# A seven-product form of the second matrix product in every second block, with one of its sums formed in place by transfers

## The chip, the cores and the metric

The kernel runs on one core of a Trainium2 chip. The metric is device time in microseconds (us) of one execution. Lower is better.

## The reference

`x` has 8 sequences of 4096 tokens with 192 features. A causal convolution of seven taps over the tokens, with softmax weights for each of 8 heads (24 features each), is followed by a two-layer network with an exact GELU and no bias:

```python
w = softmax(weight, axis=-1)                       # 8 x 7
x_unf = x_pad[:, arange(S)[:, None] + arange(7)]   # six zeros ahead of each sequence
h = einsum('hk,bskhg->bshg', w, x_unf)             # 32768 x 192
out = gelu(h @ w_in) @ w_out                       # 192 -> 2048 -> 192
```

Inputs and output are float32; the matrix products run in bfloat16.

## The kernel before

The 32768 tokens are two halves of 16384, and the kernel walks both at the same time: partitions 0 to 63 hold a third of the 192 features for the one half, partitions 64 to 127 for the other. A block `n` is 512 tokens of each half (256 in the first six), so there are 35 blocks. Every matmul from block 7 on works on 64x64 tiles, four of which run side by side on the 128x128 array. One call on each of the four tiles with 512 columns is called a *round* here.

The order on each engine is written by hand, and semaphores tie the engines together:

- **SyncE (SP)** loads `x` into three buffers `xin` and stores `osb`, in one list: load of a block ahead, store of the block before.
- **VectorE (DVE)** transposes the input (`trans`, L735), makes the taps of the convolution (`conv`, L756 and L763: `acc = xT * w + acc`, the last one into `xc` in bfloat16), and brings results out of PSUM by transposing them into `osb` (`evac_t`, L371). A tap is two calls, over 1024 and over 512 elements. The list `plan` has these steps of a block, and `side` sets other work between them: a step with the key (b, o, r) comes ahead of step o of block b.
- **ScalarE (ACT)** makes GELU, 16 calls of 1024 elements a block (slots, L910), each from one of two PSUM buffers `hp` into `gT`. For some blocks (`K0`) it also makes the first tap, in three calls (`first_tap`, L878) two blocks ahead, at the slots in `TAPS`.
- **TensorE (PE)** alternates in each slot of block `n` three rounds of the first product (`mm1`, L1005) and about three of the second product of block `n - 1` (L1085), so that a block has 48 + 48 rounds. `mm1` of a slot waits until the GELU of two slots before is done with its buffer.
- **GpSimd (POOL)** copies the halo of six tokens and issues the transfers of the sums.

In the blocks in `ST` (9, 12, ... 33) the second product has another form. Two token groups, pairs of chunks and two of the three output thirds make a 2x2x2 product, formed with seven products (P1 to P7) instead of eight; the last third (units D and E) is formed as before. So it takes 44 rounds (`A(h, par)` is the GELU output of token group h, for the chunks of parity par). It is in `mm2_s` (L1147), which follows the list `EVENTS`, made from `TILES`: a string for each of the four tiles, in which each unit (P1 to P7, D, E) is eight calls. `ROUNDS` says how many rounds stand in each slot. The form needs four sums of GELU outputs in bfloat16: S1, Dn, S4 and a quarter of S3 by DVE (`st_add`, L479 to L487), and three quarters of S3 by transfers (`st_dma`, L461 and L464: a copy into `sst`, then a second transfer that adds to it). The four PSUM banks in `ob` are called X, D, Y and V there. When products are done, ACT copies parts of X to SBUF (`st_copy`, L507, at `AT_COPY`), DVE makes corrections (`st_post`, L516 to L531) and transposes the results (`st_evac`, L543). In the block after a rewritten one, when TensorE makes these products, ACT makes copies and no first taps; DVE then makes the first tap of the block after next itself.

Of the kernel before, what the change touches and what calls it, by code (L numbers as in the profile page):

```python
# [11 lines left out]
def bass_lightweight_conv__then__act_gelu_exact_kernel(  # L12
# [80 lines left out]
    for m in range(M0, M1):  # L93
        if m in ST:
            BK[m] = dict(zip(("X", "D", "Y", "V"), FREE))
            FREE = [BK[m][k] for k in ("X", "V", "D", "Y")]
        else:
            BK[m] = FREE[:3]
            FREE = [FREE[3], *FREE[:3]]
# [22 lines left out]
    with es:  # L122
# [20 lines left out]
        wst = sbt("wst", [128, 4 * NF // 2 * 64], BF16)  # L143
        wot = sbt("wot", [128, NF * C], BF16)
        wtf = sbt("wtf", [128, NF // 2 * 64], F32)
        sst = [sbt("sst%d" % i, [128, NF // 2 * TB], BF16) for i in range(4)]
# [40 lines left out]
        S_SA = [sem("S_SA%d" % i) for i in range(4)]  # L187
        S_AC = sem("S_AC")
        S_DP = sem("S_DP")
        S_CP = [sem("S_CP%d" % q) for q in range(3)]  # L190
        S_AD = [sem("S_AD%d" % q) for q in range(3)]
# [61 lines left out]
        NCV = 2 * KS  # L253
# [29 lines left out]
        def cvd(n):  # L283

            return sum(NCV - 2 * (m in K0) for m in range(n + 1) if m not in PC)
# [15 lines left out]
        def wait_ev(e, m, g):  # L301

            if m < NA:
                e.wait_ge(S_EVA, G0[m] + g + 1)
            else:
                e.wait_ge(S_EV, EVC[m] + g + 1)

        def wait_banks(t, m, g):

            k = G0[m] + g  # L310
            if m < M0:
                if k >= 2:
                    t.wait_ge(S_EVA, k - 1)
            elif g % 2:
                t.wait_ge(S_GELU, SL0[NB] - 1 + g // 2)
            elif M1 - 1 in ST:
                i = ST.index(M1 - 1)
                t.wait_ge(*((S_AC, 6 * i + 4) if g == 0 else (S_EV, EVC[M1] - 2)))
                t.wait_ge(S_DP, 5 * i + 3 + g)
            else:  # L320
                t.wait_ge(S_EV, EVC[M1] - 2 + g)
# [42 lines left out]
        def evac_t(v, m, j):  # L364
# [8 lines left out]
        LO, UP = slice(0, 64), slice(64, 128)  # L373
        UNIT = {
# [3 lines left out]
        }  # L378
# [4 lines left out]
        NS, NE = ("S1", "S3", "Dn", "S4"), ("P1", "P5", "P7", "P3L", "P3U", "P6", "DE")  # L383

        EVENTS = []
        for (hf, cg), names in TILES.items():
            at = 0.0
            for u in names.split():
                d = 0.5 if u == "P3" else 1.0
                EVENTS += [(at + d * k / 8, hf, cg, u, k) for k in range(8)]  # L390
                at += d
        EVENTS.sort()
        GROUP = {}
        for e, (at, hf, cg, u, k) in enumerate(EVENTS):
            name = "DE" if u[0] in "DE" else u if u != "P3" else u + "LU"[cg]
# [3 lines left out]
        for e, (at, hf, cg, u, k) in enumerate(EVENTS):  # L399
# [4 lines left out]
            last[UNIT[u][0], cg] = e  # L404
        DONE = sorted(DONE)
        assert DONE[-1] < len(EVENTS) - 1
# [3 lines left out]
        def st_done(e, m, name):  # L410
            e.wait_ge(S_ST, len(DONE) * ST.index(m) + DONE.index(GROUP[name]) + 1)
# [4 lines left out]
        def weights(v, k):  # L416
# [6 lines left out]
            def w(i):  # L423
                return ap(wst, i * (NF // 2) * 64, [[4 * NF // 2 * 64, 128], [64, NF // 2], [1, 64]])
# [20 lines left out]
            elif k == 7:  # L445
                ins = v.tensor_tensor(w(3), b(1, 0), f, ALU.subtract)
            else:
                ins = v.tensor_tensor(w(2), b(0, 1), b(1, 1), ALU.subtract)
            ins.then_inc(S_WT)

        PART = {"S1": 4, "S3": 4, "Dn": 2, "S4": 2}
        ND = 3

        def st_dma(e, m, q, h):

            i, n = ST.index(m), NF // 2 // PART["S3"]
            dst = ap(sst[1], q * n * TB, [[NF // 2 * TB, 128], [TB, n], [1, TB]])
            src = ap(gT[m % 2], (4 * q * n + h) * TB, [[NF * 2 * TB, 128], [4 * TB, n], [1, TB]])
            if h == 0:
                e.wait_ge(S_GELU, SL0[m] + 2 * (q + 1) * n - 1)  # L460
                e.dma_start(dst, src).then_inc(S_CP[q], 16)  # L461
            else:
                e.wait_ge(S_CP[q], 16 * (i + 1))
                e.dma_start(dst, src, accum_op=ALU.add).then_inc(S_AD[q], 16)  # L464

        def st_add(v, m, name, q):

            g, n = gT[m % 2], NF // 2 // PART[name]

            def a(h, par):  # L470
                return ap(g, (2 * q * n + par) * 2 * TB + h * TB, [[NF * 2 * TB, 128], [4 * TB, n], [1, TB]])

            def t(k):
                return ap(sst[k], q * n * TB, [[NF // 2 * TB, 128], [TB, n], [1, TB]])

            i = ST.index(m)
            v.wait_ge(S_GELU, SL0[m] + 2 * (q + 1) * n)
            if name == "S1":
                ins = v.tensor_tensor(t(0), a(1, 0), a(1, 1), ALU.add)  # L479
            elif name == "S3":  # L480
                ins = v.tensor_tensor(t(1), a(0, 0), a(1, 0), ALU.add)
            elif name == "Dn":
                v.wait_ge(S_SA[0], PART["S1"] * i + (q + 1) * n * PART["S1"] // (NF // 2))
                ins = v.tensor_tensor(t(2), a(0, 0), t(0), ALU.add)
            else:
                v.wait_ge(S_SA[2], PART["Dn"] * i + q + 1)
                ins = v.tensor_tensor(t(3), a(0, 1), t(2), ALU.add)  # L487
            ins.then_inc(S_SA[NS.index(name)])

        def st_copy(a, m, k):  # L490

            def xb(r, w=TB):
                return bank(BK[m]["X"], r, w)

            if k > 3:
                a.wait_ge(S_AC, 6 * ST.index(m) + 4)
            if k in (0, 1, 3):
                st_done(a, m, ("P1", "P5", "", "P6")[k])
            dst, src = (
                (gsm[LO, :], xb(LO)),  # L500
                (p5s[UP, :], xb(UP)),
                (p5s[LO, 0 : TB // 2], xb(UP, TB // 2)),
                (uu[LO, :], xb(LO)),
                (uu[UP, :], uu[LO, :]),
                (gsm[UP, :], uu[LO, :]),
            )[k]
            a.activation(out=dst, in_=src, func=AF.Copy, scale=-1.0 if k > 3 else 1.0).then_inc(S_AC)  # L507

        def st_post(v, m, k):
            i = ST.index(m)  # L510
            hw = TB // 2
            vb = [bank(BK[m]["V"], r, hw) for r in (LO, UP)]
            if k == 0:
                st_done(v, m, "P7")
                v.wait_ge(S_AC, 6 * i + 2)
                ins = v.tensor_tensor(tq[UP, :], bank(BK[m]["Y"], UP), p5s[UP, :], ALU.subtract)  # L516
            elif k == 1:
                st_done(v, m, "P3L")
                v.wait_ge(S_AC, 6 * i + 3)
                ins = v.tensor_tensor(tq[LO, 0:hw], vb[0], p5s[LO, 0:hw], ALU.add)  # L520
            elif k == 2:
                st_done(v, m, "P3U")
                ins = v.tensor_tensor(tq[LO, hw:TB], vb[1], p5s[UP, hw:TB], ALU.add)
            elif k == 3:
                v.wait_ge(S_AC, 6 * i + 5)
                v.wait_ge(S_DP, 5 * i + 3)
                ins = v.tensor_tensor(tq[:, :], tq[:, :], uu[:, :], ALU.add)
            else:
                v.wait_ge(S_MM2, MMC[m + 1])
                v.wait_ge(S_AC, 6 * i + 6)  # L530
# [3 lines left out]
        def st_evac(v, m, j):  # L534
            i = ST.index(m)
            if j == 2:
                st_done(v, m, "DE")
                v.wait_ge(S_OUT[m % 2], OUTS[m - 2])
                src = bank(BK[m]["D"])
            else:  # L540
                v.wait_ge(S_DP, 5 * i + 5 - j)
# [15 lines left out]
        def store(e, m):  # L557
# [28 lines left out]
        TAPS = (7, 10, 12)  # L586
        AT_ST = {
            "S1": [(1, 9, 0), (2, 0, 0), (2, 1, 0), (2, 5, -1)],
            "S3": [(2, 5, 1)],
            "Dn": [(2, 0, 2), (2, 5, 2)],  # L590
            "S4": [(2, 0, 4), (2, 6, 0)],
            "post": [(2, 11, 0), (3, 0, 0), (3, 2, 0), (3, 6, 0), (3, 9, 0)],
            "ev": [(3, 10, 0), (3, 7, 0), (3, 4, 0)],
        }

        def at_ev(n):

            if n - 1 in ST:
                return [(2, 15, 0), (3, 4, 0), (3, 4, 0)]
            return [(2, 13, 0) if n == M0 else (3, 0, 3), (3, 5, 0), (3, 5, 0)]  # L600

        AT_COPY = {0: (1, 6), 1: (1, 8), 2: (1, 10), 3: (1, 13), 4: (2, 1), 5: (2, 4)}

        @block.gpsimd
        def _(g):
# [72 lines left out]
            for n in range(3, M1 + 2):  # L678
                if n < NB:
                    halo(n)  # L680
                if n - 2 in ST:
                    for q, h in ((0, 0), (1, 0), (0, 1), (2, 0), (1, 1), (2, 1)):
                        st_dma(g, n - 2, q, h)

        @block.vector
        def _(v):
# [50 lines left out]
            def conv(n, k, s):  # L737

                w = WS[n]
                h = int(n in K0)  # L740
                p0, pn = (0, 2) if s == 0 else (2, 1)
                if k == h and s == 0:
# [514 lines left out]
```

## Time and profile before

| | us |
|---|---|
| median of 3 runs | 671.52 |
| lowest and highest | 671.3, 672.17 |
| the profiled execution | 671.6 |
| its span in the profile | 669.9 |
| PE busy in the span | 666.3 |
| DVE busy | 596.7 |
| ACT busy | 587.4 |
| POOL busy | 90.4 |

The span runs from the first to the last instruction that the profile shows; the time also holds what lies around it. PE is TensorE's matmuls, PEld its weight loads, which overlap with them. A row of a view names the line in the kernel, the engine, the operation, the tiles as out<-in, and the shape.

### The profile page before, as it was taken

The numbers are of one execution on the slowest core, as the hardware profiler recorded it, in microseconds if no ns is written. First come the engines' busy times: TensorE is split into PE (matmuls) and PEld (weight loads), VectorE is DVE, ScalarE is ACT, GpSimd is POOL, SyncE is SP. The second block draws the span as 40 slices with busy tenths as digits, with TensorE's granted clock in tenths as the row PEclk, the third lists the DMA queues.
The fourth block names the chain that finished last, engine by engine and source line by source line (L and its number), as shares of the span: only waits on it lengthen the run. The fifth ranks groups of instructions, "written<-read, shape, count | busy, mean of one in ns | idle before, by whom it ended". The sixth has DMA issues, their size and how long they took to land.

```text
span 669.9 us, 27227 instructions
## 1 busy us (share of the span) xinstructions
PE 666.3 (99%) x12504; PEld 407.7 (61%) x12504; DVE 596.7 (89%) x706; ACT 587.4 (88%) x659; POOL 90.4 (13%) x115
## 2 busy tenths in 40 slices
PE   9999999999999999999999999999999999999998
PEld 8999655556555555655565555556555655555567
DVE  5989999899999989998999999999999999998633
ACT  8988988889988998998899889888989998898783
POOL 7020000030012003001300120030013001200300
PEclk9999999999999999999999999999999999999999
DMA  9535234263466048515634660475156346602423
GB/s 150 125 88 130 61 72 96 69 134 88 96 138 143 10 96 175 112 38 129 135 84 97 141 141 7 96 175 112 42 134 131 80 97 141 144 4 64 115 63 96
DMA packets 142786, 67.82 MB, mean 101 GB/s; under 512 B 127248, under 2 KB 140880, under 8 KB 142672
## 3 DMA queue, kind: packets, MB, share of 16 engines
q1 hardware_dynamic: 129136, 49.37, 32.6%
q0 software_dynamic: 12416, 16.13, 12.0%
q8 instruction: 98, 1.61, 1.0%
q10 hardware_dynamic: 1120, 0.59, 0.3%
q14 instruction: 16, 0.13, 0.1%
HBM read 28.31 MB, written 25.17 MB: 80 GB/s over the span
## 4 chain that ended last, share of the span: by engine, by line
PE 96%; DVE 1%; ACT 1%; DMA 1%; POOL 1%; issue 0%; POOLq 0%
PE hp L1005 48%; PE ob L1085 29%; PE ob L1147 13%; PE ob L1045 4%; PE ob L1203 1%; PE hp L1203 1%; DMA win<-in_moe_w_in_dram 1%; ACT gT L910 0%; DVE xT L735 0%; DVE acc L763 0%; POOL win L608 0%; ACT acc L878 0%; PE ob L947 0%; DVE wot L433 0%; POOL xTb L268 0%
## 5 line engine op out<-in xcount | busy, mean ns | idle before, releaser
L910 ACT ACTIVATE gT<-hp 128x1024 bf16<-128x1024 f32 x510 | 517.8, 1022 | 69.0 <-PE hp L1005 61.1
L1005 PE MATMUL hp<-xc,win 64*64 64x512 bf16 (+2 forms) x6036 | 417.7, 366 | 0.3
L763 DVE SCALAR_TENSOR_TENSOR acc<-xT,wcol,acc 128x1024 f32<-128x1024 f32 (+1 forms) x330 | 301.3, 968 | 10.7 <-ACT acc L878 10.6
L1005 PEld LDWEIGHTS hp<-xc,win 64*64 64x64 bf16 (+1 forms) x6036 | 193.7, 106 | 128.8 <-ACT gT L910 1.0
L1085 PE MATMUL ob<-gT,wot 64*64 64x512 bf16 x3648 | 248.8, 376 | 0.0
L1085 PEld LDWEIGHTS ob<-gT,wot 64*64 64x64 bf16 x3648 | 107.5, 107 | 89.4
L1147 PE MATMUL ob<-gT,wot 64*64 64x512 bf16 x864 | 109.5, 376 | 0.0
L1147 PE MATMUL ob<-sst,wst 64*64 64x512 bf16 x432 | 89.0, 376 | 0.0
L735 DVE STREAM_TRANSPOSE xT<-xin 128x1536 f32<-128x1536 f32 (+2 forms) x39 | 74.8, 1925 | 8.3 <-DMA xin<-in_x_dram 8.0
L658 POOL COPY xT<-xT 128x18 f32<-128x18 f32 x30 | 27.5, 917 | 329.7 <-DVE xc L763 168.7
L763 DVE SCALAR_TENSOR_TENSOR xc<-xT,wcol,acc 128x1024 bf16<-128x1024 f32 (+1 forms) x66 | 62.4, 970 | 0.3
L1147 PEld LDWEIGHTS ob<-gT,wot 64*64 64x64 bf16 x864 | 45.0, 107 | 26.2
L878 ACT ACTIVATE acc<-xT,wcol 128x512 f32<-128x512 f32 (+1 forms) x63 | 43.7, 693 | 0.7 <-DVE xT L735 0.7
L461 POOL DMA_DIRECT2D sst<-gT x27 | 19.7, 731 | 178.6 <-ACT gT L910 178.6
L371 DVE STREAM_TRANSPOSE osb<-ob 128x512 f32<-128x512 f32 x57 | 38.7, 710 | 4.9 <-PE ob L1085 4.3
L1045 PE MATMUL ob<-wout,gT 64*128 64x192 bf16 x768 | 41.6, 243 | 0.0
L1147 PEld LDWEIGHTS ob<-sst,wst 64*64 64x64 bf16 x432 | 36.2, 107 | 7.3
L1147 PE MATMUL ob<-gT,wst 64*64 64x512 bf16 x144 | 39.7, 376 | 0.0
L1045 PEld LDWEIGHTS ob<-wout,gT 64*128 64x128 bf16 x768 | 34.2, 94 | 4.2
L479 DVE TENSOR_TENSOR sst<-gT 128x1024 bf16<-128x1024 bf16 x36 | 25.1, 697 | 12.9 <-ACT gT L910 12.8
L464 POOL DMA_DIRECT2D sst<-gT x27 | 33.1, 1227 | 8.1 <-DMA sst<-gT 8.0
L1147 PE MATMUL ob<-sst,wot 64*64 64x256 bf16 x288 | 30.8, 269 | 0.0
(76 smaller groups left out, 262.6 us busy)
## 6 DMA issues: line engine op xcount, KB each, us to landing
out_dram<-osb SPq DMA_DIRECT2D x124, 192.0 KB, 3.3
xin<-in_x_dram SPq DMA_DIRECT2D x116, 192.0 KB, 4.2
sst<-gT POOLq DMA_DIRECT2D x54, 256.0 KB, 4.2
xin<-in_x_dram SPq DMA_DIRECT2D x18, 96.0 KB, 2.6
wout<-in_moe_w_out_dram POOLq DMA_DIRECT2D x4, 192.0 KB, 4.6
win<-in_moe_w_in_dram POOLq DMA_DIRECT2D x4, 96.0 KB, 4.4
win<-in_moe_w_in_dram POOLq DMA_DIRECT2D x2, 192.0 KB, 5.0
xin<-in_x_dram POOLq DMA_DIRECT2D x4, 96.0 KB, 4.1
```

What stands on the lines that cost most here:

```text
L371: v.transpose(osb_t(m, j), bank(BK[m][j])).then_inc(S_EV)
L464: e.dma_start(dst, src, accum_op=ALU.add).then_inc(S_AD[q], 16)
L479: ins = v.tensor_tensor(t(0), a(1, 0), a(1, 1), ALU.add)
L658: g.tensor_copy(dst, src).then_inc(S_HALO)
L735: v.transpose(out, src).then_inc(S_TR)
L763: ins = v.scalar_tensor_tensor(dst, src, wk, a, op0=ALU.mult, op1=ALU.add)
L878: a.activation(out=acc[n % 2][:, p * TB : p * TB + w], in_=ap(xT[n % 2], p * XW + HX, [[NP * XW, 128], [1, w]]), func=AF.Copy, scale=wcol[ ...
L910: a.activation(out=ap(gT[n % 2], i * c * 2 * w, dst), in_=ap(ob, 2 * TB, [[4 * TB, 128], *src[1:]]) if u < SL0[1] and u % 3 == 2 else ap(h ...
L1005: ins = t.matmul(hbuf(u, slice(fo, fo + fw), o, w), ap(win, f1, [[NP * F, 64], [2, fw]]), xc[n % 2][r, p * TB : p * TB + w], start=(p == 0 ...
L1045: ins = t.matmul(bb[sub], gT[m % 2][r, c0 : c0 + 128], wout[r, CH[sub][i] * C : (CH[sub][i] + 1) * C], start=(ph == 0 and k == 0), stop=(p ...
L1085: ins = t.matmul(bank(BK[m][j], slice(64 * h, 64 * h + 64), w), ap(wot, 64 * hf * NF * C + CH[h][i] * C + 64 * j, [[NF * C, 64], [1, 64]]) ...
L1147: ins = t.matmul(bank(BK[m][bk], slice(64 * cg, 64 * cg + 64), w), wt_, a[r, c0 : c0 + w], start=(e == mine[0]), stop=(e in (mine[-1], GRO ...
```

## The change

- `ST` is now every odd block from 9 to 33: thirteen in the place of nine. `K0` holds every block from 9 on, so ACT makes the first tap for all of them (slots 4, 8 and 12, or 2, 4 and 10 in the block whose second half carries a rewritten product).
- A tap is one call over 1536 elements (`CALLS`); only a first tap on DVE is still two. Each tap waits for the one before.
- DVE's input transpose of block n+1 stands at the head of block n's steps. Sums, corrections and output transposes stand between the taps, by the list `AT_ST` and by `at_ev`.
- S3 is formed in place. For three quarters of it a transfer adds `A(0, 0)` onto `A(1, 0)` in `gT`, in two transfers (512 and 256 KB), which wait for S1, since S1 reads `A(1, 0)`; DVE adds the last quarter in place. GELU writes a rewritten block's `gT` in four contiguous quadrants, so all sums read and write contiguous rows.
- The units change: E1 uses S1 and a new difference of weights (`wst` gets a fifth part), and the E units are split by columns, 384 in bank D (E1, E2) and 128 in bank V (e1, e2). P3 has 512 columns and goes to bank X. `TILES` and the order of the banks change with it.
- ACT makes seven copies for a rewritten block instead of six, one of them ("e") from bank V to bank D. DVE makes three corrections instead of five.
- A table `release` says, for each bank, which step frees it, and TensorE waits for that step.
- SP loads four blocks ahead in its list, not three. Weight preparation on DVE has a tenth step and moves from blocks 5, 6, 7 to 5, 7, 8.

```diff
-    ST = [m for m in range(M0 + 3, M1) if m % 3 == 0]
-    K0 = {n: i for i, n in enumerate([4, 5, 6, *(n for n in range(9, NB) if n - 3 not in ST)])}
+    ST = [m for m in range(M0 + 3, M1) if m % 2 == 1]
+    K0 = {n: i for i, n in enumerate([4, 5, 6, *range(9, NB)])}
...
-        NCV = 2 * KS
+        CALLS = {
+            n: [(0, 0, 2), (0, 2, 1)] * (n not in K0) + [(k, 0, NP) for k in range(1, KS)]
+            for n in range(NB)
+            if n not in PC
+        }
...
         UNIT = {
-            "D1": ("D", 0, 0), "D2": ("D", 0, 1), "E1": ("D", 1, 0), "E2": ("D", 1, 1),
-            "P1": ("X", 0, 0), "P6": ("X", 0, "Dn"), "P2": ("Y", 0, 1),
-            "P5": ("X", 1, "S1"), "P7": ("Y", 1, "S3"), "P4": ("Y", 1, 1), "P3": ("V", None, "S4"),
+            "D1": ("D", "A", 0, 0, "W2", 0), "D2": ("D", "A", 0, 1, "W2", 1),
+            "E1": ("D", "S1", None, None, "W2", 0), "E2": ("D", "A", 1, 1, "wst", 4),
+            "e1": ("V", "S1", None, None, "W2", 0), "e2": ("V", "A", 1, 1, "wst", 4),
+            "P1": ("X", "A", 0, 0, "W0", 0), "P6": ("X", "Dn", None, None, "wst", 1),
+            "P2": ("Y", "A", 0, 1, "W0", 1),
+            "P5": ("X", "S1", None, None, "wst", 0), "P3": ("X", "S4", None, None, "W1", 1),
+            "P7": ("Y", "S3", None, None, "wst", 2), "P4": ("Y", "A", 1, 1, "wst", 3),
         }
+        SPAN = {"E1": (HA, HB_), "E2": (HA, HB_), "e1": (0, HA), "e2": (0, HA)}
         TILES = {
-            (0, 0): "P1 D1 D2 P3 P6 P2", (1, 0): "D1 P1 P3 P6 P2 D2",
-            (0, 1): "P5 P7 E1 P3 P4 E2", (1, 1): "E1 P5 P7 E2 P3 P4",
+            (0, 0): "P1 D1 e2 e1 D2 P6 P2", (1, 0): "D1 P1 P2 e2 e1 D2 P6",
+            (0, 1): "P5 P7 E2 E1 P4 P3", (1, 1): "E2 P7:2 P5 P7:6 P3 E1 P4",
         }
...
+        COPIES = ("p5", "p1", "e", "u", "p3", "-u", "-g")
+        AT_COPY = {
+            "p5": (1, 6), "p1": (1, 8), "e": (1, 14), "u": (2, 0), "p3": (2, 2), "-u": (2, 6), "-g": (2, 10),
+        }
...
+        SUMS = {"S1": (0, 4, 6, 8), "S3": (6, 8), "Dn": (0, 4, 8), "S4": (0, 4, 8)}
...
+        AT_ST = [
+            (2, 1, 0, "S1", 0), (2, 1, 2, "Dn", 0), (2, 1, 4, "S4", 0), (2, 1, 6, "S1", 1),
+            (2, 2, 2, "S1", 2), (2, 2, 4, "S3", 0), (2, 3, 0, "Dn", 1), (2, 4, 0, "S4", 1),
+            (2, 5, 0, "k0", 0), (3, 1, 0, "ev", 2),
+            (3, 6, 0, "k3", 0), (4, 1, 1, "ev", 1), (4, 1, 5, "k4", 0), (4, 2, 0, "ev", 0),
+        ]
+        def at_ev(n):
+            return [(3, 1, 3), (3, 2, 1), (3, 2, 3)]
...
+        def st_dma(e, m, q):
+            k, k1 = SUMS["S1"][q : q + 2]
+            e.wait_ge(S_SA["S1"], sa(m, "S1", k))
+            e.dma_start(
+                quad(m, 1, 0, k, k1 - k), quad(m, 0, 0, k, k1 - k), accum_op=ALU.add
+            ).then_inc(S_AD[q], 16)
...
-        TAPS = (7, 10, 12)
+        TAPS = ((4, 8, 12), (2, 4, 10))
...
-                if k == h and h:
-                    v.wait_ge(S_K0, NP * K0[n] + p0 + pn)
-                elif idx >= 2:
-                    v.wait_ge(S_CV, idx - 1)
+                if c == 0 and n in K0:
+                    v.wait_ge(S_K0, NP * (K0[n] + 1))
+                elif k > 0:
+                    v.wait_ge(S_CV, idx)
...
                 if n + 1 in K0:
-                    ops[6 if n < 6 else 2 : 6 if n < 6 else 2] = [("t", n + 1, 0)]
+                    k = 2 if n < 7 else int(n not in K0)
+                    ops[k:k] = [("t", n + 1, 0)]
...
+                if FIRST[bk, cg] == e and REL[m, BK[m][bk]]:
+                    need(*REL[m, BK[m][bk]])
...
             for n in range(1, NB):
-                if n + 3 < NB:
-                    load(sp, n + 3)
+                if n + 4 < NB:
+                    load(sp, n + 4)
                 store(sp, n - 1)
```

More of the change, by code (lines that the diff above doesn't have):

```diff
@@ L283, in cvd @@
         def cvd(n):
-            return sum(NCV - 2 * (m in K0) for m in range(n + 1) if m not in PC)
+            return sum(len(CALLS[m]) for m in range(n + 1) if m not in PC)
         def xin_at(n):
@@ L466, in st_add @@
[L466 to L474, printed above, removed]
-            i = ST.index(m)
[L477 to L507, printed above, removed]
```

346 lines of the change are left out of this document (196 added, 150 removed).

## The prediction

> **What bounds the kernel now.** I read the page first, then the windows, the chain of waits in order of time, the groups by shape in a steady stretch, and the timelines of each engine.
>
> ```profile
> span 669.9 us, 27227 instructions
> PE 666.3 (99%) x12504; PEld 407.7 (61%) x12504; DVE 596.7 (89%) x706; ACT 587.4 (88%) x659; POOL 90.4 (13%) x115
> ...
> PEclk9999999999999999999999999999999999999999
> ...
> PE 96%; DVE 1%; ACT 1%; DMA 1%; POOL 1%; issue 0%; POOLq 0%
> ```
>
> TensorE is the bound: 99% busy at full granted clock, and 96% of the chain that ended last. The windows, in 61 us (three blocks), and the chain say the same of the middle of the run:
>
> ```profile
> 411.00:472.00 61.00, 61.00 (x1152) 34.54 (x1148) 57.47 (x65) 54.58 (x60) 7.92 (x9) 1.00 0.48 106
> ```
>
> ```profile
> 352.19 0.65 PE ob L1085 x12
> ...
> 356.08 0.86 PE ob L1085 x16
> ...
> 376.80 0.86 PE ob L1085 x16
> ...
> 417.38 0.86 PE ob L1085 x16
> ```
>
> The columns of the window row are busy time of PE, PEld, DVE, ACT and POOL. DVE is at 57.47 of 61 (94%), ACT at 54.58 (89%): both have little room. In the chain, twelve calls take 0.65 and sixteen take 0.86. Four 64x64 tiles run side by side, so one round of four calls takes 0.216. The x16 rows at 356.08, 376.80 and 417.38 are the same slot of three plain blocks. The first two are one plain block apart: 20.72, which is 96 rounds (48 of the first product, 48 of the second). The last two have a plain and a rewritten block between them: 40.58, so the rewritten one took 19.86, which is 92 rounds. Nothing else shows in either: a block costs its rounds. So one more rewritten block is worth 0.86 to the end, as long as TensorE never waits.
>
> **The gain.** The rewritten blocks go from nine (9, 12, ... 33) to thirteen (9, 11, ... 33). The form still has 44 rounds: four more blocks give 4 x 0.86 = 3.4 us.
>
> **What the new form costs TensorE.** P3 was of 256 columns in each tile column; it is 512 wide now, and E is split into 384 columns (E1, E2) and 128 (e1, e2). Sixteen 128-column calls follow one another on one tile, twice in a block, beside wider calls on the other three. The nearest rows are the 256-column calls of P3, and the 128-column calls of the start:
>
> ```profile
> 341.87 0.27 PE L1147 MATMUL ob<-sst,wot 64*64 64x256 bf16 x2
> ...
> 342.63 0.27 PE L1147 MATMUL ob<-sst,wot 64*64 64x256 bf16 x2
> ```
>
> ```profile
> L947 PE MATMUL ob<-xTb,dg 64*64 64x128 bf16 x28 | 0.9, 216 | 0.0
> ```
>
> Eight calls of P3 follow one another on a tile from 341.87 to 342.63: 0.109 each, half a round. The 28 calls of L947 run as 14 pairs on two tiles: (0.9 - 0.16 of the last one's tail) / 13 = 0.057 each. Sixteen at 0.056 are 0.90 where four rounds are 0.86: 0.03, twice, so 0.07 in a block and 0.8 us in thirteen. From the other side, if each call waited for the one before it to end, it would take its 0.216, and the block would grow by 5 us. I take 0.056: same shape, same engine, weights also changed at each call. The net of TensorE is 3.4 - 0.8 = 2.6 us. The Trainium skill (TensorE: Matmul & The Clock Gate, Back-to-back issue gap) has about 81 ns for N=128 with a weight load before each matmul; L947 above has such loads and shows 57, though on two tiles alone. By 81 the two runs would take 0.87 more in a block and the change would end at 679.9.
>
> **DVE.** A pair of blocks now has one plain block and one rewritten. Rows in the steady stretch, by shape:
>
> ```profile
> L910 ACT ACTIVATE gT<-hp 128x1024 bf16<-128x1024 f32 x197 | 200.1, 1021 | 26.8 <-PE hp L1005 23.5
> L763 DVE SCALAR_TENSOR_TENSOR acc<-xT,wcol,acc 128x1024 f32<-128x1024 f32 x63 | 80.6, 1279 | 0.0
> L763 DVE SCALAR_TENSOR_TENSOR acc<-xT,wcol,acc 128x512 f32<-128x512 f32 x63 | 47.2, 749 | 3.3 <-ACT acc L878 3.3
> L735 DVE STREAM_TRANSPOSE xT<-xin 128x1536 f32<-128x1536 f32 x12 | 27.8, 2316 | 2.9 <-DMA xin<-in_x_dram 2.8
> L371 DVE STREAM_TRANSPOSE osb<-ob 128x512 f32<-128x512 f32 x26 | 17.6, 707 | 0.4 <-PE ob L1085 0.2
> L878 ACT ACTIVATE acc<-xT,wcol 128x512 f32<-128x512 f32 x24 | 17.1, 712 | 0.0
> L479 DVE TENSOR_TENSOR sst<-gT 128x1024 bf16<-128x1024 bf16 x16 | 11.1, 695 | 2.3 <-ACT gT L910 2.3
> L484 DVE TENSOR_TENSOR sst<-gT,sst 128x2048 bf16<-128x2048 bf16 x8 | 9.8, 1220 | 0.4
> L531 DVE TENSOR_TENSOR gsm<-ob,gsm 128x512 f32<-128x512 f32 x4 | 2.7, 684 | 0.0
> ```
>
> ```profile
> 336.40 3.80 DVE L763 SCALAR_TENSOR_TENSOR acc<-xT,wcol,acc 128x1024 f32<-128x1024 f32 x4
> 340.11 1.27 DVE L763 SCALAR_TENSOR_TENSOR xc<-xT,wcol,acc 128x1024 bf16<-128x1024 f32 x1
> ```
>
> ```profile
> 658.11 0.69 DVE L527 TENSOR_TENSOR tq<-tq,uu 128x512 f32<-128x512 f32 x1 [0.57 <-ACT uu L507]
> 658.84 0.71 DVE L543 STREAM_TRANSPOSE osb<-tq 128x512 f32<-128x512 f32 x1
> 659.47 0.65 DVE L531 TENSOR_TENSOR gsm<-ob,gsm 128x512 f32<-128x512 f32 x1
> ```
>
> 512 elements more cost 1.279 - 0.749 = 0.53, so a call over all 1536 is 1.81. L543 at 658.84 reads what L527 made and starts 0.04 after its end; L531 at 659.47 needs nothing of its neighbour and starts 0.08 before its end. So a single tap directly behind the tap that it needs costs 1.85, no less than the two calls before (336.40 to 340.11, two taps: 1.855 each). With other work between, it costs 1.73. Five of twelve taps in a pair stand behind their producer, seven do not. The pair: 12 taps x 1.81, 2 input transposes x 2.32, five sums of 2048 x 1.21, three of 1024 x 0.695, six output transposes x 0.71, three corrections x 0.69: 40.8 in 31 calls. Twenty-four overlaps of 0.08 and seven gaps of 0.04 (the five taps, and the two transposes that now stand right behind the last tap whose input they overwrite) make 39.2, against 19.92 + 20.72 = 40.64 of TensorE: 96%. It fits since ACT now makes the first tap of every block from 9 on; eight of them lose their two calls of it on DVE.
>
> The sum alone doesn't decide; the order does. I put the calls of one pair in their written order with these prices, zero being where TensorE starts the block that carries the rewritten block's second product. DVE's last point of rest is the correction k3, which needs the negated copy that ACT makes behind gelu 5 of the next block: 19.92, then 6.67 to slot 5 (four slots of six rounds, one of seven), 1.9 until its gelu is done (ACT's rows below: 413.3 for slot 0 of the block whose slot 4 shows at 417.38 and which starts 6.0 ahead of that), 0.65 for the copy, so 29.1, and 0.1 to DVE. From there DVE has k3 0.60, a tap 1.73, the input transpose 2.35, S1 1.13, ev 0.63, Dn 1.13, evict 0.63, S4 1.12, k4 0.60, S1 0.61, a tap 1.73, ev 0.63, evict 0.63, and the last quarter of S1, 0.69: 14.2, so 43.4. TensorE first wants that quarter (P5, k=6) in slot 2 of the next rewritten block: 40.64 + 2.59 + 0.65 - 0.2 for its weight load = 43.7. It fits by 0.3 us. The other appointments have more: bank D by its eviction, 1.1; k0 for P4, 0.8; bank Y by k4, 2.2.
>
> **ACT.** It gains eight blocks of first taps, and the copies go from six to seven a rewritten block (two of 64x512 in the place of one of 64x256, one of 64x128 new).
>
> ```profile
> 402.07 0.59 ACT L507 ACTIVATE p5s<-ob 64x512 f32<-64x512 f32 x1
> 402.69 1.94 ACT L910 ACTIVATE gT<-hp 128x1024 bf16<-128x1024 f32 x2
> ...
> 413.30 0.63 ACT L507 ACTIVATE uu<-uu 64x512 f32<-64x512 f32 x1
> ```
>
> Two gelus in 1.94 are 0.92 apart when none waits (the second is 1.02 long); a tap adds 0.61, a copy 0.5 to 0.8. A pair: 32 x 0.92 + 6 x 0.61 + 7 x 0.64 = 37.6 of 40.64, 93%. Locally, the p5 copy moves to slot 6, behind a slot of only five rounds (1.08). It adds 0.59 + 0.05 and the 0.10 by which two gelus overlap, 0.74, so that gelu 6 starts 0.74 + 0.92 - 1.08 = 0.58 late and ends 1.9 + 0.58 = 2.48 after its slot's start; slot 8, which needs its buffer, starts at 2.59. The largest lateness before is 0.42 (the negated copy, 0.79 + 0.92 - 1.29), and TensorE shows none of it. I count 0.05 here, 12 times: 0.6 us.
>
> **Transfers.** The S3 sum was a copy and an accumulating transfer of 256 KB each, three times; now two accumulating ones, in place, of 512 and 256 KB.
>
> ```profile
> sst<-gT POOLq DMA_DIRECT2D x54, 256.0 KB, 4.2
> ```
>
> ```profile
> DMA  0059999999999501014999999999950000000000
> ...
> sst<-gT POOLq DMA_DIRECT2D x1, 256.0 KB, 3.6
> ```
>
> The first row is the whole run's median to landing, the other two are the window from 450 to 455: each 256 KB accumulate keeps the 16 engines full for twelve slices of 0.125, 1.5 us, and lands 3.6 after its issue. Twice the bytes: 3.6 + 1.5 = 5.1. POOL issues it when S1's first half is done, at 35 in the count above, so it lands at 40.1; with the median of 4.2, most of them beside loads, doubled, at 43.4. P7 wants it at 43.7, as P5 wants its quarter. SP holds each rewritten block's store for its last eviction (ev0, 42.7 in the count), and the loads queue behind: they come after. So it costs nothing; each us beyond that cover is one a pair. The loads of x move a block ahead in SP's order, with the input transposes that use them; with three buffers, a load still waits for a transpose three blocks back, done long before. Behind the last block the same evictions and stores follow, at the same cost.
>
> **Sum.** 671.6 of the profiled run (1.7 more than its span; the median of the three runs is 671.5) - 3.4 + 0.8 + 0.6 - 0.2 = 669.4. The last term is the start, of which this is the row from 13 to 69:
>
> ```profile
> PEld hp L1005 <- ACT gT L910: 0.9, 3, 0.4
> ```
>
> Three times the weight loads wait for a gelu, in blocks 4 and 5; at a round of 0.216 before the calls themselves stop, under 0.3 of that is left to win. The input transpose of block 6, on which those gelus hang, comes a tap earlier now, and three weight calls leave block 6 for 7. I take 0.2. The forecast's own range is 667.6 (short calls and ACT cost little) to 670.2.
>
> **The rivals.** (1) DVE is late for P5. It has 0.3 us, and the chain of 14.2 us is priced by addition; at 0.5 us more than I count the gain of 2.2 is gone (0.2 x 12), at 1 us more each pair loses 0.7, and it ends at 677.8: slower. For it: 96% load, and transposes that now wait for the last tap. Against: each piece was seen at its price, and the wait before k3 absorbs what goes wrong earlier. (2) The short calls don't fill their tile: a 128-column call issued behind a 512-column one cannot end before it. Then, of the four short calls of a round, the second ends with the wide one at 0.216 and two more follow at 0.057: a round of 0.33 for eight rounds, 0.9 a block, 11.9 in all in place of the 0.8, and 680.5. It makes the change slower from 0.061 us a call (the two runs then eat 0.23 a block). For it: short calls were never seen beside three busy tiles. Against: P3's calls kept 0.109 beside 512-column ones, though as they end with them that hardly tests it. The Trainium skill (TensorE: Matmul & The Clock Gate, What overlaps and what doesn't) states this order: matmuls end in the order of the program. (3) ACT's lateness of 0.58 costs 0.1 to 0.2 a pair and not 0.05: 670.5, no change to be measured. (4) The larger transfer lands 2 us late: 12 x 2, 693.
>
> **The numbers.** Forecast 0.64, rival 1 0.14, rival 2 0.09, rival 3 0.08, rival 4 0.05. A measurement here can tell 0.2%, 1.3 us: faster is under 670.2. Faster: 0.64 and a third of rival 3, with the smallest of rival 1: 0.69; same 0.10; slower 0.21. The range goes from 667.6, and up to 673, into the milder half of rival 1, which leaves out about 2 in 10.
>
> **What would show it.** Right: rewritten blocks of 19.9 and plain ones of 20.72 alternating, PE still 99%, DVE idle only before k3 and the D eviction, S1's last quarter done within 3 us of a block's start. Wrong: PE waiting for a DVE sum at P5 (rival 1), rewritten blocks of over 20.3 with no wait (rival 2), gelu behind copies (3), PE waiting for gT by DMA at P7 (4).

## The result and the profile after

The changed kernel takes 668.17 us (median of 5; 667.87 to 669.77) against 671.59 us before (median of 5; 671.3 to 672.17). The ratio is 0.9954, with a 95% interval of 0.994 to 0.9969. The prediction was 669.4, from 667.6 to 673.0.

The page of the changed kernel, by its span, its busy times, the granted clock and the chain that ended last:

```profile
span 666.1 us, 27567 instructions
PE 661.4 (99%) x12712; PEld 516.4 (78%) x12712; DVE 600.7 (90%) x510; ACT 610.8 (92%) x720; POOL 47.6 (7%) x87
...
PEclk9999999999999999999999999999999999999999
...
PE 99%; ACT 0%; DVE 0%; DMA 0%; issue 0%; ACTq 0%
...
gT<-gT POOLq DMA_DIRECT2D x13, 512.0 KB, 4.6
gT<-gT POOLq DMA_DIRECT2D x13, 256.0 KB, 3.3
```

TensorE is still the bound; its share of the chain went from 96% to 99%. DVE makes its work in 510 calls instead of 706, ACT is 23 us busier, and POOL has 26 transfers to issue instead of 54. The profiled execution took 667.87, 1.8 more than its span.

Where the 3.8 us of span came from is read from two points of the chain in order of time: the first slot of block 7 with 16 calls of the second product, and the first 32 calls on `hp` of the closing product (the second product of the last block). First the kernel before, then the changed one:

```profile
90.13 0.86 PE ob L1085 x16
...
659.53 2.64 PE hp L1203 x32
```

```profile
89.05 0.86 PE ob L1150 x16
...
333.52 0.86 PE ob L1150 x16
...
374.13 0.86 PE ob L1150 x16
...
414.73 0.86 PE ob L1150 x16
...
655.29 2.64 PE hp L1258 x32
```

- The start, up to block 7: 90.13 to 89.05, so 1.08 shorter.
- The middle: 569.40 between the two points before, 566.24 after, so 3.16 shorter. The rows at 333.52, 374.13 and 414.73 are the same slot of three plain blocks, one pair of a plain and a rewritten block apart each: 40.61 and 40.60, where the one such pair before was 40.58. So a rewritten block lost 0.02 against the old form, and four more of them gave the rest.
- The tail: 669.9 - 659.53 = 10.37 before, 666.1 - 655.29 = 10.81 after, 0.44 longer, behind the last matmul. From TensorE's last matmul to the end of the span it is 2.9 here, 2.4 before. The kernels of the experiments that keep this tail as it is have 2.4 (experiments 1 and 9) to 3.6 (experiment 4): it varies, and no run shows why.

The window of one such pair, and what DVE waits for from 160 to 640:

```profile
408.68:449.29 40.61, 40.61 (x791) 32.68 (x785) 39.20 (x32) 38.46 (x46) 2.46 (x4) 1.00 0.45 99
```

```profile
DVE tq L608 <- ACT uu L598: 11.4, 12, 1.0
...
```

DVE is busy for 39.20 us of the pair's 40.61, the figure of the forecast. Twelve times, once a pair, it rests for just under 1 us: at k3 (L608), for ACT's negated copy. That is the point of rest of the forecast, and from it the timeline of DVE shows the chain of which all depended:

```profile
377.40 0.69 DVE L608 TENSOR_TENSOR tq<-tq,uu 128x512 f32<-128x512 f32 x1 [0.96 <-ACT uu L598]
378.01 1.81 DVE L827 SCALAR_TENSOR_TENSOR xc<-xT,wcol,acc 128x1536 bf16<-128x1536 f32 x1
379.91 2.41 DVE L800 STREAM_TRANSPOSE xT<-xin 128x1536 f32<-128x1536 f32 x1
382.26 1.17 DVE L559 TENSOR_TENSOR s_S<-gT 128x2048 bf16<-128x2048 bf16 x1
...
388.02 1.80 DVE L827 SCALAR_TENSOR_TENSOR acc<-xT,wcol,acc 128x1536 f32<-128x1536 f32 x1
389.75 0.69 DVE L624 STREAM_TRANSPOSE osb<-gsm 128x512 f32<-128x512 f32 x1
390.38 0.66 DVE L373 STREAM_TRANSPOSE osb<-ob 128x512 f32<-128x512 f32 x1
390.98 0.64 DVE L559 TENSOR_TENSOR s_S<-gT 128x1024 bf16<-128x1024 bf16 x1
```

From k3's start at 377.40 to the end of S1's last quarter (L559 at 390.98, plus 0.64) there are 14.2 us, as worked out. Block 22 of TensorE starts at 388.79, so the quarter is there 2.82 after that.

### The profile page after: what moved, and what is told of

It is laid out like the page before. It is cut to its first block, busy times and chain, and to the rows that moved or that the text cites. A ratio compares the mean times of both kernels' runs of the same rounds, so it can differ in the third digit from the quotient of the medians.

```text
span 666.1 us, 27567 instructions
## 1 busy us (share of the span) xinstructions
PE 661.4 (99%) x12712; PEld 516.4 (78%) x12712; DVE 600.7 (90%) x510; ACT 610.8 (92%) x720; POOL 47.6 (7%) x87
## 4 chain that ended last, share of the span: by engine, by line
PE 99%; ACT 0%; DVE 0%; DMA 0%; issue 0%; ACTq 0%
PE hp L1066 50%; PE ob L1150 23%; PE ob L1202 18%; PE ob L1106 5%; PE ob L1258 1%; PE hp L1258 1%; PE ob L1011 0%; DMA wsb<-in_weight_dram 0%; PE ob L1066 0%; ACT dg L912 0%; DVE wcol L772 0%; ACT xc L237 0%; ACT osb L347 0%; ACT wex L899 0%; ACT xTb L269 0%
## 5 line engine op out<-in xcount | busy, mean ns | idle before, releaser
L1066 PEld LDWEIGHTS hp<-xc,win 64*64 64x64 bf16 (+1 forms) x6036 | 247.2, 106 | 73.0 <-ACT gT L974 4.6
L827 DVE SCALAR_TENSOR_TENSOR acc<-xT,wcol,acc 128x1536 f32<-128x1536 f32 (+1 forms) x165 | 282.9, 1714 | 10.6 <-ACT acc L938 7.3
L1202 PE MATMUL ob<-gT,wst 64*64 64x512 bf16 (+2 forms) x832 | 144.0, 323 | 0.0
L1202 PE MATMUL ob<-s_S,wot 64*64 64x128 bf16 (+2 forms) x624 | 89.9, 305 | 0.0
L1202 PEld LDWEIGHTS ob<-gT,wst 64*64 64x64 bf16 x832 | 68.5, 107 | 10.7
L827 DVE SCALAR_TENSOR_TENSOR xc<-xT,wcol,acc 128x1536 bf16<-128x1536 f32 (+1 forms) x33 | 56.7, 1720 | 0.8
L1202 PE MATMUL ob<-s_S,wst 64*64 64x512 bf16 x208 | 57.4, 376 | 0.0
L1202 PE MATMUL ob<-s_Dn,wst 64*64 64x512 bf16 x208 | 57.4, 376 | 0.0
L1202 PEld LDWEIGHTS ob<-s_S,wot 64*64 64x64 bf16 x624 | 50.2, 107 | 8.6
L545 POOL DMA_DIRECT2D gT<-gT x26 | 22.4, 861 | 318.1 <-DVE s_S L559 318.1
L559 DVE TENSOR_TENSOR s_S<-gT 128x1024 bf16<-128x1024 bf16 (+1 forms) x39 | 32.6, 837 | 1.4 <-ACT gT L974 1.3
```

The lines of the kernel that those rows point to most:

```text
L545: e.dma_start(quad(m, 1, 0, k, k1 - k), quad(m, 0, 0, k, k1 - k), accum_op=ALU.add).then_inc(S_AD[q], 16)
L559: ins = v.tensor_tensor(t("S1"), quad(m, 1, 0, k, n), quad(m, 1, 1, k, n), ALU.add)
L827: ins = v.scalar_tensor_tensor(dst, src, wk, a, op0=ALU.mult, op1=ALU.add)
L1066: ins = t.matmul(hbuf(u, slice(fo, fo + fw), o, w), ap(win, f1, [[NP * F, 64], [2, fw]]), xc[n % 2][r, p * TB : p * TB + w], start=(p == 0 ...
L1202: ins = t.matmul(bank(BK[m][bk], slice(64 * cg, 64 * cg + 64))[:, c0 : c0 + w], wt_, x, start=(e == mine[0]), stop=(e == mine[-1] or e in ...
```

## The experiments

**1. The old set of blocks, everything else new.**

```diff
-    ST = [m for m in range(M0 + 3, M1) if m % 2 == 1]
+    ST = [m for m in range(M0 + 3, M1) if m % 3 == 0]
```

> The changed kernel with the rewritten form in every third block from 9 on, the nine blocks of before; single taps, new form, start and order stay. Theory (the gain is four more blocks of four rounds, 0.83 each by the changed kernel's own blocks, plus a shorter start): 668.2 + 4 x 0.83 = 671.5, about the time before, 671.6, since start (-1.1), tail (+0.4) and 9 x 0.02 of the form nearly cancel to -0.5: between 671.1 and 671.5. The recorded price of short calls and p5's copy (0.07 + 0.05 a rewritten block, start -0.2): 672.4. Rival (the gain comes from the single taps and the order of DVE, which free TensorE of small waits): it stays near 668.2.

Measured: 671.01 (670.64 to 672.17), ratio to before 0.9995 (0.9986 to 1.0004). The two points of the chain in this kernel:

```profile
89.13 0.86 PE ob L1150 x16
...
658.70 2.64 PE hp L1258 x32
```

With nine rewritten blocks the gain is gone. The middle takes 569.57, where it took 569.40 before and takes 566.24 with thirteen. So the gain of the middle comes from the number of rewritten blocks, 3.3 us for four of them by these points (2.8 by the medians), and not from single taps or from DVE's order. What is left of this kernel's lead, about 0.6, is its start, which is 1.0 shorter. The recorded price of short calls and copy, which would have given 672.4, is too high.

**2. The start alone, in the kernel before.**

```diff
-                    ops[6 if n < 6 else 2 : 6 if n < 6 else 2] = [("t", n + 1, 0)]
+                    k = 4 if n in (4, 5) else 2
+                    ops[k:k] = [("t", n + 1, 0)]
-    ((M0 - 1 + k // NP, 2 * k + 1, 0), weights, v, k)
+    ((M0 - 1 + (k >= NP) * (2 + (k - NP) // 4), 2 * k + 1 if k < NP else 4 + 2 * ((k - NP) % 4), 0), weights, v, k)
```

> The kernel before with only the start of the change: the input transposes of blocks 4 to 6 stand as many taps ahead as in the change, and the weight sums leave block 6 for blocks 7 and 8. Theory (this is what shortened the start; the waits in slots 0 to 4 of the block at 50 to 57 us, 0.75 in all, go): 671.6 - 0.75 = 670.8. Rival (the single calls of the taps are what lets these transposes be early): 671.4 to 671.6. The recorded value of the start was -0.2.

Measured: 671.11 (670.47 to 671.75), ratio 0.9987 (0.9978 to 0.9996): 0.5 less by the medians. It is real, and larger than the 0.2 of the prediction. The chain of the kernel before shows what is gone, in block 4 of TensorE (46.61 to 57.85):

```profile
48.27 2.21 DVE xT L735
...
50.50 0.72 ACT acc L878
51.22 0.92 ACT gT L910
...
52.19 0.83 PE hp L1005 x12
...
53.71 0.83 PE hp L1005 x12
...
56.53 0.83 PE hp L1005 x12
```

and the chain of this kernel, which stays on PE there:

```profile
50.71 0.66 PE hp L1006 x12
51.37 0.66 PE ob L1046 x16
52.03 0.66 PE hp L1006 x12
...
89.40 0.86 PE ob L1086 x16
```

Before, the chain leaves TensorE: an input transpose holds a first tap on ACT, which holds a gelu, on which TensorE waits. Three of its slots there take 0.83 + 0.66 instead of 0.66 + 0.66, and block 4 takes 11.24, with the new start 10.52. The same slot of block 7 comes at 89.40 with the new start, at 90.13 without: 0.73. The other 0.35 of the changed kernel's 1.08 lies ahead of block 2, which starts at 25.57 in both of these kernels and at 25.20 in the changed one. Among variants of the changed kernel below with the same work up to there, it starts between 25.13 and 27.75, so the 0.35 is not put down to the change.

**3. Two calls a tap again.** `conv` makes each tap from the second on as 1024 and 512 elements, each waiting only for the call two before it; all positions stay.

```diff
-                elif k > 0:
-                    v.wait_ge(S_CV, idx)
+                for s, (p0, pn) in enumerate([(0, 2), (2, 1)] if k > 0 else [(p0, pn)]):
+                    conv1(n, k, c, s, idx + s, p0, pn)    # waits for S_CV >= idx + s - 1
```

> The changed kernel with each tap from the second on made in two calls again (1024 and 512 elements, each waiting only for the call two before it), everything else in its place. Two taps lie in the chain from k3 to the last quarter of S1, and each costs 1.855 in place of 1.73 there: 0.25 a pair more. Theory (the chain has 0.1 to 0.3 to spare, by the trace): 668.2 to 670.0. If the chain had no room at all: 668.2 + 12 x 0.25 = 671.2. Rival (DVE is not near the path): 668.2. If the sum of DVE decides (seven taps a pair dearer by 0.12, 40.0 of 40.6): 668.2 too.

Measured: 669.75 (669.25 to 670.84), ratio 0.9973 (0.9961 to 0.9984). A pair's window has DVE at 40.13 of 40.60:

```profile
409.81:450.41 40.60, 40.60 (x789) 33.29 (x784) 40.13 (x44) 38.46 (x46) 2.58 (x4) 1.00 0.45 99
```

```profile
PEld hp L1077 <- ACT gT L985: 3.6, 20, 0.2
PEld ob L1213 <- DVE s_S L559: 0.9, 1, 0.9
PEld ob L1161 <- DVE osb L624: 0.2, 1, 0.2
```

```profile
299.56 2.94 DVE L800 STREAM_TRANSPOSE xT<-xin 128x1536 f32<-128x1536 f32 x1
```

It almost fits: TensorE waits noticeably for S1 in one pair of twelve (its block grew by 0.85), where the input transposes took 2.94 and 3.0 instead of 2.3 to 2.4 and DVE had hardly any rest left to take that in; in another pair, with transposes of 2.54 and 2.59, the block grew by 0.1. So the single calls make the room for such a step (0.93 a pair: 40.13 against 39.20); without them the change would still win, by less.

**4 to 6. One DVE call more, in three places.** A 128x512 multiply-add of a buffer that is free by then, once or twice for each rewritten block; the output is unchanged.

```diff
-            (3, 6, 0, "k3", 0), (4, 1, 1, "ev", 1), (4, 1, 5, "k4", 0), (4, 2, 0, "ev", 0),
+            (4, 1, 0, "dm", 0), (3, 6, 0, "k3", 0), ...                       # behind k3
+            (3, 4, 0, "dm", 0), (3, 6, 0, "k3", 0), ...                       # ahead of k3
+            (4, 1, 0, "dm", 0), (4, 1, 7, "dm", 1), (3, 6, 0, "k3", 0), ...   # two behind k3
```

> The changed kernel with one more DVE call for each rewritten block (a 128x512 multiply-add of a scratch buffer, about 0.75 long, 0.67 with the overlap), placed behind k3, in the chain that ends with S1's last quarter. Theory of the order (the prediction's 0.3 us to spare; in the changed kernel that quarter is done 2.8 after the block's start, and with two-call taps TensorE showed a wait from about 3.2 on, so 0.35 to 0.4): 0.27 to 0.35 late in each of 12 pairs, 668.2 + 3.2 to 4.2 = 671.4 to 672.4. Theory of the sum alone (DVE rests 0.96 a pair, 0.67 fits in): 668.2.

> The same extra call, placed two taps ahead of k3, before DVE's point of rest. Theory of the order: the 0.96 us that DVE waits at k3 for the negated copy takes it in, 668.2. If what matters is DVE's load and not the place: the same time as with the call behind k3.

> Two such calls behind k3, 1.34 in all. Theory of the order: 1.34 - 0.37 = 0.97 late in each of 12 pairs, 668.2 + 11.6 = 679.8. Theory of the sum: 39.65 + 1.34 = 40.99 of DVE in a pair of 40.61 of TensorE, 0.38 over, 12 x 0.38 = 4.6: 672.8.

Measured: behind k3 670.94 (670.3 to 672.25; ratio 0.9986, 0.9977 to 0.9996); ahead of k3 669.07 (668.41 to 670.5; ratio 0.9961, 0.9947 to 0.9975); two behind k3 678.71 (677.48 to 679.87; ratio 1.0102, 1.0082 to 1.0121). What TensorE's weight loads wait for between 160 and 630, with one call behind, one ahead, and two behind:

```profile
PEld ob L1210 <- DVE s_S L560: 3.0, 11, 0.3
```

```profile
PEld hp L1074 <- ACT gT L982: 3.8, 21, 0.2
PEld ob L1210 <- DVE s_S L560: 0.2, 1, 0.2
```

```profile
PEld ob L1210 <- DVE s_S L560: 10.3, 11, 1.0
```

The place decides, not the load. From the first call of block 7 to the first of block 34, TensorE takes 549.4 in the changed kernel, 549.6 with the call ahead of k3, 551.5 with one behind and 558.8 with two. Ahead of k3 the call disappears into the wait at k3; one pair there is late all the same, by 0.2, and its input transposes took 2.93 and 2.96. Behind k3, the call makes S1's last quarter late in eleven of the twelve pairs (the first of them has no k3 ahead of it), and the second call there costs its full length: the wait grows by 0.66 a pair, which is the second call's own step in the chain (14.77 to 15.43). The sum's forecast for two calls was 672.8; it took 678.7. With one call, 670.94 lies between the forecasts and 0.5 under that of the order, since a late block grew by 0.19 and not by 0.27 to 0.35. The quarter ended 3.37 after the start of TensorE's block with one call, and slot 2 grew by 0.10; so TensorE wants it by about 3.27, and the 2.82 of the changed kernel has about 0.45 to spare. Slots 6 and 7 of a block that was held up in slot 2 grew by 0.10 together, whatever the length of the wait; I did not find why.

**7. S3 on DVE, without transfers.**

```diff
-        SUMS = {"S1": (0, 4, 6, 8), "S3": (6, 8), ...}
+        SUMS = {"S1": (0, 4, 6, 8), "S3": (0, 4, 6, 8), ...}
-            (2, 2, 4, "S3", 0)
+            (2, 1, 3, "S3", 0), (2, 1, 7, "S3", 1), (2, 2, 4, "S3", 2)
-                    for q in range(2):
-                        st_dma(g, n - 2, q)
```

> The changed kernel with the whole S3 sum on DVE: two more in-place sums (2048 and 1024 elements, 1.13 and 0.61 with the overlap) a rewritten block, behind S1's first half and its third quarter, and no transfers. Both stand in the chain between k3 and S1's last quarter. Theory of the order (that chain has 0.45 to spare, worked out from the runs with an extra call): 1.74 - 0.45 + 0.1 = 1.4 late in each of 12 pairs, 668.2 + 16.7 = 684.9. Theory of the sum alone: 39.65 + 1.74 = 41.39 of DVE against 40.61: 0.78 x 12 = 9.4, 677.6. If the transfers themselves were what is late or in the way: less than 668.2.

Measured: 685.21 (684.77 to 685.49), ratio 1.0201 (1.0187 to 1.0214), on the forecast of the order (684.9) and 7.6 above that of the sum.

```profile
PEld ob L1199 <- DVE s_S L559: 17.0, 11, 1.6
```

Two sums that DVE could almost hold by its load (39.2 + 1.7 of 40.6) cost 17 us where they stand, 16.1 of them in eleven pairs. The transfers carry them at no time: in the changed kernel POOL issues the 512 KB transfer at 383.73, it lands 4.6 later in the median, and P7 wants it beside P5 at about 392.

**8 and 9. Short calls by themselves.** In the 15 plain blocks from 6 on (the expectations below count 16), one tile's call (then: two tiles') is made as four calls of 128 columns, in all 48 rounds of the second product.

```diff
+                        n = 4 if (hf, h) == (0, 0) else 1      # two tiles: if h == 0
+                        for z in range(n):
+                            ... columns z * w // n to (z + 1) * w // n of the same call
```

> The changed kernel, where in each of the 16 plain blocks from 6 on the call on one of the four tiles (rows 0 to 63, lower columns) is made as four calls of 128 columns with the same weights, in all 48 rounds of the second product: 768 rounds in which four short calls follow one another beside three wide ones. By the prediction's 0.056 a call, a round of 0.224 in place of 0.216: 6.1 us more, 674.3. By what the changed kernel's rewritten blocks show (0.02 a block of 32 short calls and p5's copy together, at most 0.0547 a call): under 2 us, 670.2. By the rival of the prediction, that a short call cannot end before the wide call issued ahead of it: 0.33 a round, 88 us, 756. By 81 ns a call, which the Trainium skill (TensorE: Matmul & The Clock Gate, Back-to-back issue gap) has for 128 columns with a weight load ahead of each: 0.324 a round, 83 us, 751.

> As with short calls on one tile in the plain blocks (21.08 a block, 674.2), but on two tiles: rows 0 to 63 and rows 64 to 127 of the lower columns, four calls of 128 columns each in every round. Theory (a tile's short calls lengthen only its own round, and tiles run side by side, so two tiles cost what one costs; it is why the rewritten block grew by 0.02 and not by twice 0.03): 21.08 a block again, 674.2. Rival (the cost of short calls adds over the tiles, in the issue of the calls): 21.44 a block, 16 x 0.36 more, 680.

Measured: one tile 674.19 (673.62 to 675.17; ratio 1.0039, 1.0026 to 1.0052), two tiles 676.42 (676.34 to 677.04; ratio 1.0072, 1.0058 to 1.0086). The chain, in the same slot of two plain blocks with a rewritten one between, for one tile and for two:

```profile
336.49 0.86 PE ob L1153 x16
...
377.46 0.86 PE ob L1153 x16
```

```profile
339.70 0.84 PE ob L1153 x27
...
380.67 0.84 PE ob L1153 x28
```

Both pairs take 40.97, 0.36 more than the changed kernel's 40.61. That is 0.0075 for each of 48 rounds: 0.2234 for four short calls, 0.0559 a call. The price of the prediction, 0.056, holds beside three busy tiles, and two tiles with short calls in the same rounds cost what one costs. The 670.2 read from the changed kernel's own blocks did not come. By the 81 ns that the Trainium skill (TensorE: Matmul & The Clock Gate, Back-to-back issue gap) states for N=128 with weight loads, the round would be 0.324 and the pair some 45.8; the runs here show 55.9 ns a call. By the Trainium skill's rule that matmuls end in the order of the program (same page, The mechanism, What overlaps and what doesn't) a round would have taken 0.33; no such wait appears for calls on different tiles.

The 2.2 us more of the two-tile kernel aren't in its later pairs, but in blocks 7 and 8, which take 21.9 and 22.4 there and 21.1 each with one tile. Between 84 and 130 its TensorE stands still twice for nothing that the profile shows:

```profile
PE ob L1153 <- issue: 1.7, 2, 1.1
```

All four executions of this kernel lie within 0.7 us, so this looks like a cost of the kernel and not a chance of one execution; what causes it stays open.

**10 to 12. One more rewritten block, 7.** First by the set alone, `range(M0 + 1, M1)`. Then also with the weight work in two waits of DVE at the start, and block 7's first sums and block 6's first eviction ahead of an input transpose. Then with S1's last quarter and two evictions a tap earlier there.

```diff
-    ST = [m for m in range(M0 + 3, M1) if m % 2 == 1]
+    ST = [m for m in range(M0 + 1, M1) if m % 2 == 1]
...
-        SIDE += [((M0 - 1, 2 * k + 1, 0) if k < NP else (M0 + 1 + (k - NP) // 4, 2 + (k - NP) % 4, 0), "w", 0, k) ...]
+        SIDE += [((5, 0, 0) if k < 7 else (6, 0, 0), "w", 0, k) ...]                           # second and third
-                return [(3, 1, 3), (3, 2, 1), (3, 2, 3)]
+                return [(3, 0, 3), (3, 2, 1), (3, 2, 3)]                                       # second
+                return [(3, 0, 3), (3, 1, 1), (3, 1, 3)]                                       # third
-                SIDE += [((n + d, o, r), name, n, q) for d, o, r, name, q in AT_ST]
+                SIDE += [((n + d, o - (n == 7 and (d, o) == (2, 1)), r), name, n, q) ...]      # second
+                SIDE += [((n + d, o - (n == 7 and (d, o) in ((2, 1), (2, 2))), r), ...) ...]   # third
```

> The changed kernel with block 7 rewritten too, the odd blocks from 7 to 33: fourteen. Theory (each rewritten block is worth 0.83 as long as TensorE never waits): 667.3. Rival (blocks 7 and 8 still have their first tap on DVE, two calls more each, 1.85, and the weight sums of the start fall there; DVE is late for the first rewritten block): 668.2 to 670.

> The changed kernel with block 7 rewritten too, and DVE's work at the start set for it: the three weight copies and the first four weight sums go into the 3.2 us that DVE waits at 41.7, the last three into the 0.7 us at 54, and the first sums of block 7 stand a tap earlier, with the first eviction of block 6. Theory (the block from 104 to 127 lost 3.45 because DVE was 3.5 late there, and this frees 3.2 of weight work and puts the 2.3 of an input transpose behind the sums): block 8 back at 19.9, 668.2 - 0.83 = 667.3. Rival (the first pair has too much on DVE even so, since blocks 7 and 8 have their first tap on it): 668.5 to 670.

> As the last kernel with block 7 rewritten (weight work in DVE's waits at 41.7 and 54, the first sums of block 7 ahead of an input transpose), and also the last quarter of S1, the rest of S3 and two evictions of block 6 one tap earlier there. In the kernel before this one the block from 103.7 lost 0.84, by S1's last quarter, which ended at 107.7 behind a tap of 1.78; now it should end at 106.2. Theory: block 8 at 19.9, 668.2 - 0.83 = 667.3. Rival (another of DVE's appointments of block 8 is late next, as the evictions or Dn's second half): no gain, 668.2 to 668.7.

Measured: 670.81 (670.31 to 671.36), 668.68 (667.83 to 669.52) and 668.06 (667.73 to 668.92; ratio 0.9949, 0.9936 to 0.9963). What TensorE waits for in the stretch of block 8, in its weight loads in the first two kernels and in its matmuls in the third:

```profile
PEld ob L1202 <- DVE s_S L559: 2.4, 2, 2.1
PEld ob L1202 <- DVE osb L373: 1.5, 1, 1.5
```

```profile
PEld ob L1202 <- DVE s_S L559: 0.9, 1, 0.9
```

```profile
PE ob L1202 <- DVE tq L604: 0.2, 1, 0.2
```

The first pair carries first taps and weight work that the later ones don't. Its block lost 3.45 us at first, then 0.84, then 0.39, now by the correction k0 (L604), and with that the gain of 0.83 is down to nothing that the runs can tell from the changed kernel (668.17). Each repair showed the next late step; my forecast of 667.3 did not come.

## Why the prediction was right, and where its terms were off

- **The bound, and four blocks fewer by four rounds (-3.4).** Right. The pair is 40.61, and the old set of blocks gives the time back (experiment 1).
- **Short calls (+0.8).** The step that failed is "0.03, twice, so 0.07 in a block". The 0.056 a call was right (0.0559 in experiment 8), but it was a measure of one tile, and I added it over tiles that run side by side. In the same rounds, two tiles cost what one does (experiment 9). The change has its two runs in different slots, 6 and 7 on one tile and 9 on the other, and there too the second costs next to nothing: in the rewritten blocks of experiment 8, slot 6 takes 1.317 instead of 1.295, and slot 9 takes 1.515, where the seven rounds of a plain slot take 1.511. That the second tile makes up then for what the first lost is argued, not shown. One run's 0.03 was due; the block grew by 0.02.
- **Rival 2**, which the Trainium skill's rule (TensorE: Matmul & The Clock Gate, The mechanism, What overlaps and what doesn't) speaks for. Refuted: 674.2 where it would have been 756. The prediction gave it 0.09, and only because no trace of before had short calls beside busy tiles.
- **DVE's chain.** The step on which most hung, and it held: 39.2 busy and 14.2 us from k3, both as added up. The room was 0.45 instead of 0.3, since TensorE wants the quarter at 3.27 after its block's start and I had 3.06 (43.7 - 40.64). Rival 1 is what experiments 4, 6 and 7 made by hand: from 0.45 us on, each pair loses what goes beyond.
- **ACT's copy at slot 6 (+0.6, and rival 3).** The lateness came as priced, but costs next to nothing: gelu 6 of block 22 ends 2.53 after its slot's start (2.48 in the prediction). Weight loads wait for gelu 22 times between 160 and 630, 0.2 at most. In nine of twelve blocks with a rewritten product, slot 8, whose buffer that gelu frees, takes 1.105 instead of 1.079, and slot 9 1.51 instead of 1.52 before; three blocks lose nothing. In experiment 8 the same 0.02 stands in slot 6, at the short calls, so it can't be divided between the two. Together 1.4 was counted and 0.26 came (13 x 0.02), so the forecast's middle was 1.1 too high.

```profile
PEld hp L1066 <- ACT gT L974: 4.1, 22, 0.2
```

- **Transfers.** 5.1 from issue to landing was estimated, 4.6 is the median; no wait for `gT` by transfer appears. Right, and rival 4 did not come.
- **The start (-0.2).** The step that failed is the bound: one row of waits in the weight loads, cut to "under 0.3", stood for all that TensorE could lose there. The chain at that place shows three slots of 0.83 and DVE and ACT in it. The move brought 0.73.
- **The tail (none).** It was 0.44 longer in this profile; from kernel to kernel with the same tail it varies by more than that.

Together: forecast 669.4; short calls and ACT 1.1 less and the start 0.5 less would have made it 667.7, and 668.17 was measured. The mechanism was right; the three terms whose size was wrong all made the forecast too slow, so its middle was 1.2 above the result. The last 0.4 is no more than the tail and the spread of the runs.

## What to carry to other kernels

When an engine off the bound is laid out by hand at 96%, work out the chain between its last point of rest and the bound's next demand: that margin (0.45 us here) says what one more call costs, and it may cost nothing on the one side of the rest and its full length on the other. A cost measured on one tile should not be added over tiles that run side by side without a test. For a gain at a kernel's start, follow the chain of waits in that stretch, not only the rows that name a wait.

## What the runs showed of the hardware that was not expected

- 128-column calls on a 64x64 tile follow one another at 0.0559 us beside three tiles with 512-column calls, and short calls on a second tile in the same rounds add nothing (40.97 a pair in both).
- The 1536-element input transpose, a constant piece in the forecast, goes from 2.3 to 2.4 us along the changed kernel's execution. It took 2.94 and 3.0 in one pair of experiment 3, 2.93 and 2.96 in one of experiment 5, and about 3.0 in every block of experiment 1 from 282 us on. The same window from 280 to 600 in that kernel and in the changed one:

```profile
L800 DVE STREAM_TRANSPOSE xT<-xin 128x1536 f32<-128x1536 f32 x16 | 48.3, 3017 | 1.5
```

```profile
L800 DVE STREAM_TRANSPOSE xT<-xin 128x1536 f32<-128x1536 f32 x16 | 38.5, 2406 | 1.5
```

With two blocks in three left plain that costs TensorE nothing; against a room of 0.45, 0.6 more makes it wait, as in the late pairs of experiments 3 and 5. What makes the transpose longer stays open.
- TensorE sometimes stands still early in an execution for 0.8 to 1.1 us with no cause in the profile. In the run with a call ahead of k3 this is most of why block 7's slot comes at 91.61, where the changed kernel has 89.05 with the same work ahead of it:

```profile
PE ob L1074 <- issue: 1.1, 1, 1.1
PE ob L1114 <- issue: 0.8, 1, 0.8
```

It is as large as several of the terms weighed here, and a reason to read the middle and the start of a profile apart.
